# Packed attention and two mixture layers on one core: the order of all operations from a table in the kernel instead of a planner's run

## The chip, the cores and the metric

The kernel runs on one core of a Trainium2 chip. The metric is the device time of one execution in microseconds (us), as a median of several runs. Profiles are of one execution. The engines are TensorE (PE in the rows, PEld for its weight loads), VectorE (DVE), ScalarE (ACT), GpSimd (POOL) and SyncE (SP). DMAs are issued from SP's queue and, for a few tensors, from ACT's.

## The reference

```python
# q, k, v: 8 x 8 x 576 x 64; p: 8 x 8 x 32 x 64
packed = softmax(p @ k.T / 8) @ v              # 32 packed rows for each head
x = softmax(q @ packed.T / 8) @ packed         # 8 x 8 x 576 x 64 -> 4608 x 512
h = x @ moe_w_in                               # 4608 x 1024
solu = h * softmax(h)
x = layernorm(solu) * moe_g_ln @ moe_w_out     # 4608 x 512
h = x @ moe2_w_in                              # 4608 x 2048
out = relu(h) ** 2 @ moe2_w_out                # 4608 x 512
```

The weights arrive as 64-bit floats, and the kernel decodes them from their bits on ACT, DVE and POOL.

## The kernel before

**Stages.** Attention goes batch by batch (`pack`, `unpack`): scores of the packed rows against k (`s`, L648), softmax (`mx`, `nmx`, `e`), transposes of `e` (`pt`, L713), the product with v (`ppp`, L724), the packed result scaled (`pp`, `pd`, L728 and L730) and transposed (`ptp`, L740 and L741) into `ppf` and `ppq`, and scores of q against it (`s` again, L648, turned by DVE into `a` at L757). The product of `a` with the packed values and w_in is made as `G` = `ppq` times w_in (`pg`, L659, copied by ACT at L525) and `h` = `aT` times `G` (`ph`, L819 and L842), by 128 tokens. `h_tile` applies the softmax, the normalisation and transposes (`ptv`, L886), and `y_stage` multiplies by w_out (`py`), 256 tokens at a time, and stores to `y_dram`. These three run interleaved up to some 480 us. Beside them `prepare` decodes the second layer's first weights, forms seven combinations of their quarters (Strassen's products) and stores them in `z_dram`. Then come the second layer's two stages: `z_group` (seven products for a group, L1087, with sums and squares in `finish`) up to some 820 us, and `o_products` (L1221) to the end. The big products are made of three fp32r matmuls each (L543 to L545).

**The beginning.** `load_w_in` loads four parts of w_in (`wraw`, 1 MB each, one row of 8 KB on each of 128 partitions), which are decoded by three ACT instructions (L558, L565, L567) and four DVE instructions (L569, L572, L574, L577). w_out comes in the same way in four parts, with eight multiplications on ACT besides (L610, `gain`). `load_turned` loads k and q in halves of 576 KB (`kr`, `qr`), which DVE transposes (L634). `p` comes in four small DMAs (`pr`, rows of 256 B), for the first batch from ACT's queue, and DVE transposes it into `pT` (L670).

**What sets the order.** `Plan.op` and `Plan.either` only record operations: 5198 of them, each with the engines that may do it, a planned time on each, an urgency, what it reads and writes. `Plan.order` then runs through them as a list scheduler, with planned times, DMA rates and free buffers, and returns the order in which they are emitted; `Plan.backward` derives urgencies from the end; `emit` repeats both 24 times, adds the 126 `NUDGES` (shifts of urgency for stretches of the list), and emits the last order. Each engine executes its instructions in the order of their emission, and SP and ACT issue their DMAs in it too. Operations given to `either` with two engines (most weight preparations: POOL or DVE; `finish`: DVE, or ACT with two instructions, L1103 and L1104) get the one that is free first. Tiles of a shared ring (PSUM's four banks `m` among them) get the slot that came free first.

```python
order = self.order()
with self.tc.manual_schedule():
    for i in order:
        self.ops[i].fn(self.ops[i].engine)
```

Of the kernel before, what the change touches and what calls it, by code (L numbers as in the profile page):

```python
# [22 lines left out]
NUDGES = (  # L23
    (1586, 1862, DVE, -1.11), (723, 1022, DVE, -1.47), (2336, 2361, DMA, 9.02), (2358, 2372, DVE, 9.56), (696, 741, PE, 4.72),
    (870, 1143, PE, -0.81), (1028, 1040, DVE, -6.49), (1783, 1837, None, 16.47), (236, 431, DVE, -0.6), (1536, 1538, None, 2.54),
    (1591, 1756, ACT, -4.01), (1484, 1626, None, -3.27), (2001, 2027, None, -13.45), (1816, 2088, DMA, -6.41), (167, 178, None, -0.94),
    (796, 835, ACT, 1.33), (1985, 2076, DMA, 3.89), (691, 739, None, -54.14), (1771, 1847, DVE, 6.28), (1995, 2049, None, -76.95),
    (480, 683, DVE, 19.6), (487, 528, DVE, -5.08), (538, 780, ACT, -17.25), (1720, 1862, ACT, -3.92), (1626, 1631, None, -25.73),
    (472, 474, ACT, -4.98), (1610, 1852, DMA, -0.72), (2269, 2346, DMA, -5.22), (1846, 2199, PE, 18.2), (2172, 2184, PE, -1.08),
    (445, 529, None, -0.5), (945, 1021, None, -1.58), (1010, 1055, DVE, 3.0), (2218, 2282, PE, 1.4), (1086, 1271, DVE, 7.73),  # L30
    (2277, 2307, DVE, -5.99), (916, 993, DMA, 25.12), (871, 887, DVE, 18.48), (1168, 1178, DVE, -2.23), (1119, 1173, DVE, -3.12),
    (860, 884, ACT, 9.92), (2188, 2193, None, -2.05), (2273, 2344, PE, 1.65), (2308, 2377, ACT, -1.56), (258, 266, DVE, -10.26),
    (2224, 2347, None, 0.59), (642, 729, None, -2.11), (2299, 2315, None, 1.75), (831, 896, DVE, 0.82), (2031, 2195, PE, 1.46),
    (2293, 2428, DVE, 9.0), (269, 385, PE, -1.52), (662, 850, DVE, -0.09), (780, 828, None, 1.11), (1736, 1763, DMA, -0.48),
    (1792, 1825, DVE, 0.4), (1374, 1423, PE, -20.54), (261, 297, None, -1.17), (335, 423, ACT, -1.17), (1137, 1417, DVE, 9.8),
    (998, 1120, DVE, 3.18), (853, 954, DVE, -1.49), (1801, 1865, None, 14.94), (452, 458, None, -9.15), (68, 112, DVE, -2.26),
    (25, 26, None, 1.6), (157, 207, DVE, 1.98), (1290, 1377, None, -3.16), (1762, 1763, None, 13.71), (1569, 1632, DVE, 3.47),
    (4, 353, PE, -1.94), (280, 289, None, 2.49), (1590, 1594, DVE, 2.4), (1896, 1995, None, 2.54), (262, 279, None, 3.07),
    (430, 463, None, 1.29), (637, 768, ACT, 36.7), (356, 378, None, -0.85), (540, 542, DVE, -2.6), (1141, 1153, DVE, -25.46),
    (1159, 1162, PE, -9.93), (333, 359, DVE, -5.17), (752, 757, None, 2.49), (882, 1114, None, 0.41), (793, 885, DVE, 8.18),  # L40
    (643, 664, None, 3.28), (966, 1002, DVE, 36.52), (93, 99, None, -5.09), (683, 706, None, 2.3), (1789, 1853, None, -11.75),
    (257, 263, None, -9.55), (235, 371, DVE, -0.85), (206, 383, None, -0.39), (440, 448, None, -3.81), (279, 432, ACT, 6.21),
    (501, 506, None, -2.21), (269, 273, ACT, 7.19), (2124, 2127, PE, -18.82), (223, 263, DVE, -5.29), (2240, 2253, None, 1.9),
    (2096, 2277, DVE, -3.83), (412, 430, DVE, 7.08), (118, 139, None, 0.28), (1764, 1793, None, 8.76), (2211, 2492, None, 9.02),
    (2270, 2298, None, 1.31), (2204, 2587, DVE, 8.62), (2401, 2457, PE, 4.01), (2112, 2113, None, 2.19),
# [75 lines left out]
class Plan:  # L121

    WINDOW = 3413.0
    FLYING = 8
    YIELD = 60.0
    SWITCH = {True: 157.0, False: 157.0}  # L130

    @staticmethod
    def hop(a, b):

        return 0 if a == b == PE else (260, 130, 110, 70, 40)[a] + (20 if b == PE else 0)

# [45 lines left out]
    def reset(self):  # L182
        for o in self.ops:
            o.engine = None
            for b in o.bufs:
                b.slot = None
                if b.ring:
                    b.ring.free = [(0.0, n) for n in range(b.ring.bufs)]

    def backward(self):  # L190

        ops, ends = self.ops, self.ends
        deps = [set(o.deps) for o in ops]
        slots = {}
        for b in dict.fromkeys(b for o in ops for b in o.bufs if b.slot is not None):
            slots.setdefault((b.ring, b.slot), []).append(b)
        for bufs in slots.values():
            bufs.sort(key=lambda b: ends[b.touched[0]])
            for a, b in zip(bufs, bufs[1:]):
                deps[b.touched[0]].update(a.touched)  # L200
        left = [0] * len(ops)
        for i, d in enumerate(deps):
            d.discard(i)
            for j in d:
                left[j] += 1
        able = [[] for _ in range(5)]
        busy = [False] * 5
        free, starts = [0.0] * len(ops), [0.0] * len(ops)
        port = 0.0
        events = [(0.0, i, "ready") for i in range(len(ops)) if not left[i]]  # L210
        heapq.heapify(events)
        while events:
            now = events[0][0]
            while events and events[0][0] <= now:
                t, i, what = heapq.heappop(events)
                e = ops[i].engine
                if what == "ready":
                    heapq.heappush(able[e], (-ends[i], i))
                    continue
                busy[e] = False  # L220
                for j in sorted(deps[i]):
                    left[j] -= 1
                    free[j] = max(free[j], t + self.hop(ops[j].engine, e) + ops[j].lag + ops[j].slack)
                    if not left[j]:
                        heapq.heappush(events, (free[j], j, "ready"))
            for e in (PE, ACT, POOL, DVE, DMA):
                if not busy[e] and able[e]:
                    _, i = heapq.heappop(able[e])
                    busy[e] = True
                    starts[i] = now + ops[i].engines[e]  # L230
                    if e == POOL or e == DVE and ops[i].port:
                        port = starts[i] = max(now, port) + ops[i].engines[e]
                    heapq.heappush(events, (starts[i], i, "free"))
        end = max(starts)
        for o, t in zip(ops, starts):
            if not o.fixed:
                o.urgency = round((end - t) / 1e3, 6)

    def order(self):
        ops = self.ops  # L240
        self.reset()
        self.ends = [0.0] * len(ops)
        users = [[] for _ in ops]
        left = [len(o.deps) for o in ops]
        able = [[] for _ in range(5)]
        busy = [False] * 5
        events = []
        uses = {}
        pe_busy, pe_warm = {}, [False]
        port = 0.0  # L250
        landed = []

        def pe_end(t, ns):

            while ns > 1e-6:
                w = int(t / self.WINDOW + 1e-9)
                while len(pe_warm) <= w:
                    share = pe_busy.get(len(pe_warm) - 1, 0.0) / self.WINDOW
                    pe_warm.append(share > 0.74 or (share > 0.5 and pe_warm[-1]))
                slow = 1 if pe_warm[w] else 2  # L260
                d = min(ns * slow, (w + 1) * self.WINDOW - t)
                pe_busy[w] = pe_busy.get(w, 0.0) + d
                t += d
                ns -= d / slow
            return t

        for i, o in enumerate(ops):
            for d in o.deps:
                users[d].append(i)
            for b in o.bufs:  # L270
                uses[b] = uses.get(b, 0) + 1
            if not o.deps:
                heapq.heappush(events, (0.0, i, "ready"))
        order = []
        mode = [False]

        def claim(i, held, now):
            need = {}
            for b in ops[i].bufs:
                if b.ring and b.ring.shared and b.slot is None:  # L280
                    need.setdefault(b.ring, []).append(b)
            for ring, bufs in need.items():
                if sum(f <= now for f, _ in ring.free) - held.get(ring, 0) < len(bufs):
                    for r, bs in need.items():
                        held[r] = held.get(r, 0) + len(bs)
# [1027 lines left out]
```

## Time and profile before

| what | us |
|---|---|
| median of 3 runs (1199.88 to 1206.17) | 1203.17 |
| the profiled execution, its own time | 1204.65 |
| its span, first to last instruction | 1202.9 |
| PE busy | 1157.2 |
| DVE busy | 885.2 |
| ACT busy | 794.6 |
| POOL busy | 143.7 |

The profiled execution's time holds 1.75 us beyond its span. Busy time of PE includes matmuls that run at a lowered clock and pipelined ends, so the rows of single stretches say more than the sum.

### The profile page before, as it was taken

Reading aid. Unit: us, or ns where it says so; the run is one execution under the profiler, and the core shown is the slowest. Engines: PE = TensorE matmul, PEld = TensorE weight load, DVE = VectorE, ACT = ScalarE, POOL = GpSimd, SP = SyncE. Lnnn points to the kernel's source line nnn. Section 1 sums busy time; section 2 is a strip of 40 time slices with the busy share of each in tenths; the row PEclk is TensorE's granted clock in tenths of the full one; section 3 lists DMA queues with packets and bytes.
Section 4 is the critical chain, followed back from the end, with each engine's and each line's share of the span. In section 5 each row is a group of like instructions: output and inputs, shape, how many; then the busy total and the mean of one; then the engine's idle time right before and its main releaser. Section 6 shows DMA issues by size and latency. Waiting matters only on the chain.

```text
span 1202.9 us, 26204 instructions
## 1 busy us (share of the span) xinstructions
PE 1157.2 (96%) x10044; PEld 1086.8 (90%) x10044; DVE 885.2 (74%) x1784; ACT 794.6 (66%) x1672; POOL 143.7 (12%) x159
## 2 busy tenths in 40 slices
PE   1789999999999999999999999999999999999998
PEld 0357988889798999999999999999999999999998
DVE  5999897897765843567767776744888888888885
ACT  5698757776666864678777878877545454545452
POOL 0112333243232740000000000000000000000000
PEclk9789999999999999999999999999999999999999
DMA  9643563473324579677575767556983626252601
GB/s 343 199 133 118 154 195 115 149 221 119 96 76 123 154 246 356 216 243 232 190 250 189 236 203 246 169 192 239 400 320 97 190 75 186 79 187 80 189 17 54
DMA packets 171079, 218.79 MB, mean 182 GB/s; under 512 B 17353, under 2 KB 133577, under 8 KB 170185
## 3 DMA queue, kind: packets, MB, share of 16 engines
q1 hardware_dynamic: 129961, 192.07, 48.4%
q10 hardware_dynamic: 40992, 25.04, 6.8%
q8 instruction: 79, 1.29, 0.4%
q14 instruction: 47, 0.39, 0.1%
HBM read 131.08 MB, written 85.98 MB: 180 GB/s over the span
## 4 chain that ended last, share of the span: by engine, by line
PE 88%; ACT 4%; DVE 4%; DMA 2%; issue 1%; POOL 0%; ACTq 0%; SPq 0%; DVEq 0%; POOLq 0%
PE px L543 10%; PE px L545 10%; PE px L544 10%; PE ph L842 8%; PE py L543 5%; PE pa L545 5%; PE pa L543 5%; PE pa L544 5%; PE py L545 5%; PE py L544 5%; PE pz L545 3%; PE pz L543 3%; PE pz L544 3%; PE ptv L886 2%; PE s L648 2%; PE pw L544 1%
## 5 line engine op out<-in xcount | busy, mean ns | idle before, releaser
L525 ACT CAST cb<-ga 128x384 fp32r<-128x384 f32 x336 | 167.8, 514 | 161.1 <-PE pa L545 69.9
L528 DVE TENSOR_TENSOR cb<-ga,cb 128x384 fp32r<-128x384 f32 x336 | 180.4, 553 | 57.7 <-ACT cb L525 56.2
L543 PE MATMUL py<-v,wo 128*128 128x256 f32 x576 | 166.3, 289 | 0.0
L545 PE MATMUL py<-v,wo 128*128 128x256 f32 x576 | 162.8, 283 | 0.0
L544 PE MATMUL py<-v,wo 128*128 128x256 f32 x576 | 162.7, 283 | 0.0
L543 PE MATMUL px<-oi,cb 128*128 128x256 f32 x504 | 142.1, 282 | 0.8 <-ACT gw L1122 0.8
L545 PE MATMUL px<-oi,cb 128*128 128x256 f32 x504 | 142.2, 282 | 0.0
L543 PE MATMUL pa<-oi,cb 128*128 128x256 f32 x504 | 142.0, 282 | 0.0
L544 PE MATMUL pa<-oi,cb 128*128 128x256 f32 x504 | 142.0, 282 | 0.0
L545 PE MATMUL pa<-oi,cb 128*128 128x256 f32 x504 | 142.0, 282 | 0.0
L544 PE MATMUL px<-oi,cb 128*128 128x256 f32 x504 | 142.0, 282 | 0.0
L543 PE MATMUL px<-y,zi 128*128 128x384 f32 x384 | 129.6, 337 | 1.4 <-ACT gw L1091 1.3
L545 PE MATMUL px<-y,zi 128*128 128x384 f32 x384 | 129.4, 337 | 0.0
L544 PE MATMUL px<-y,zi 128*128 128x384 f32 x384 | 129.4, 337 | 0.0
L1095 DVE TENSOR_TENSOR gw<-pz,gw 128x384 f32<-128x384 f32 x96 | 53.1, 554 | 86.4 <-PE pz L545 62.1
L543 PEld LDWEIGHTS py<-v,wo 128*128 128x128 f32 x576 | 110.0, 191 | 3.0 <-DVE a L757 0.9
L544 PEld LDWEIGHTS py<-v,wo 128*128 128x128 f32 x576 | 110.2, 191 | 1.1 <-issue 0.2
L545 PEld LDWEIGHTS py<-v,wo 128*128 128x128 f32 x576 | 110.1, 191 | 0.0
L1035 DVE TENSOR_TENSOR ga<-ga 128x384 f32<-128x384 f32 x192 | 100.4, 551 | 2.1 <-DMA ga<-g_dram 1.1
L543 PEld LDWEIGHTS px<-oi,cb 128*128 128x128 f32 x504 | 95.4, 189 | 1.0 <-ACT gw L1122 1.0
L545 PEld LDWEIGHTS px<-oi,cb 128*128 128x128 f32 x504 | 95.4, 189 | 0.1
L544 PEld LDWEIGHTS px<-oi,cb 128*128 128x128 f32 x504 | 95.4, 189 | 0.0
(141 smaller groups left out, 2869.5 us busy)
## 6 DMA issues: line engine op xcount, KB each, us to landing
g_dram<-gw SPq DMA_DIRECT2D x192, 192.0 KB
ga<-g_dram SPq DMA_DIRECT2D x96, 384.0 KB
zi<-z_dram SPq DMA_DIRECT2D x28, 512.0 KB
oi<-o_dram SPq DMA_DIRECT2D x24, 512.0 KB
kr<-in_k_dram SPq DMA_DIRECT2D x16, 576.0 KB
qr<-in_q_dram SPq DMA_DIRECT2D x16, 576.0 KB
vr<-in_v_dram SPq DMA_DIRECT2D x16, 576.0 KB
y_dram<-ysb ACTq DMA_DIRECT2D x72, 128.0 KB
```

Source lines behind the costliest of these rows:

```text
L525: plan.op(ACT, c_act(cols, sbuf=r[0].pool not in (psm, psh, pso)), at, lambda: nc.scalar.copy(out_(), in_()), r=r, w=w)
L528: plan.either(on(cols, *engines), at, lambda e: vec[e].tensor_tensor(out_(), in_(), hi_().bitcast(F32), op=ALU.subtract), r=r, w=w, port=i ...
L543: nc.tensor.matmul(ps, lh, rh, start=first, stop=False, skip_group_check=onto)
L544: nc.tensor.matmul(ps, lh, rl, start=False, stop=False, skip_group_check=onto)
L545: nc.tensor.matmul(ps, ll, rh, start=False, stop=last, skip_group_check=onto)
L648: nc.tensor.matmul(banks[u]()[32 * e:32 * e + 32, :SH].rearrange("p (m t) -> p m t", t=T), lhs(ps, e, f), ts[e // 2]()[ps, e % 2, :, f], s ...
L842: nc.tensor.matmul(ph()[:, fs], al[l]()[:, g], g_tiles[b, g]()[:, r, fs], start=ends[0] and g == 0 and t == 0, stop=ends[1] and g == NG - ...
L886: nc.tensor.transpose(pt()[:, c * P:(c + 1) * P], e()[:, (4 * t + c) * P:(4 * t + c + 1) * P], ident)
L1035: plan.op(DVE, c_dve(cols), at, lambda: nc.vector.tensor_tensor(out_(), in0(), in1(), op=op), r=r, w=w, port=True)
L1095: plan.op(DVE, c_dve(HN), when(p, SN), lambda: nc.vector.tensor_tensor(t(), ps()[:, :HN], t(), op=ALU.add), r=[t, ps], w=[t])
```

## The change

The scheduler (`order`, `backward`, `reset`, the constants and `NUDGES`) is gone. `ORDER` is a table of all 5198 operations in the order of their emission, and `SECOND` lists those that go to the second of the engines that they name. The list of operations, their instructions and their buffers are as before. The lines of all that follows the tables lie 13 higher.

```diff
-NUDGES = (
-    (1586, 1862, DVE, -1.11), (723, 1022, DVE, -1.47), (2336, 2361, DMA, 9.02), (2358, 2372, DVE, 9.56), (696, 741, PE, 4.72),
...
+ORDER = (
+    45, 0, 4, 6, 53, 46, 47, 5, 48, 3, 2, 1, 382, 49, 17, 50, 61, 7, 54, 51, 55, 8, 69, 52,
...
+SECOND = (
+    1773, 1774, 1776, 1778, 1791, 1792, 1795, 1807, 1808, 1824, 1842, 1844, 1861, 1863, 1892, 1927, 1929, 1943, 1944, 1945, 1960, 1962, 1963, 1965,
...
-    def emit(self, passes):
-        order = self.order()
...
+    def emit(self):
+
+        assert sorted(ORDER) == list(range(len(self.ops))), "the table is of another list"
+        second = set(SECOND)
+        free, uses = {}, {}
         for o in self.ops:
             for b in o.bufs:
+                if b.ring and b.ring.shared:
+                    uses[b] = uses.get(b, 0) + 1
+        done = set()
+        with self.tc.manual_schedule():
+            for i in ORDER:
+                o = self.ops[i]
+                assert o.deps <= done, "the table breaks a dependence"
+                for b in o.bufs:
+                    if b in uses and b.slot is None:
+                        b.slot = free.setdefault(b.ring, list(range(b.ring.bufs))).pop(0)
+                o.fn(list(o.engines)[i in second])
+                done.add(i)
+                for b in o.bufs:
+                    if b in uses:
                         uses[b] -= 1
+                        if not uses[b]:
+                            free[b.ring].append(b.slot)
...
-    plan.emit(PASSES)
+    plan.emit()
```

Against the order before, 95 operations change their engine: 37 weight preparations of the z stage go from POOL to DVE (8 at L577, 8 of 256 and 13 of 128 columns at L925, 8 at L528), 45 `finish` operations go from ACT (35 with two instructions there, 10 with one) to one instruction on DVE, and 13 go from DVE to ACT. On PE 605 of the 1072 operations stand at the same place, and an operation moves by 1.5 places in the mean; PE's last 467 operations, ACT's last 542 and DVE's last 749 are the same list in the same order.

SP's queue from its first DMA on, before (`wraw` from w_in are the four parts of w_in):

```order
L470 DMA g_sb<-in_moe_g_ln_dram 128x8x1
L512 DMA wraw<-in_moe_w_in_dram 128x2048
L512 DMA kr<-in_k_dram 128x2x576 x2
L512 DMA wraw<-in_moe_w_in_dram 128x2048
L512 DMA qr<-in_q_dram 128x2x576 x2
L512 DMA wraw<-in_moe_w_in_dram 128x2048
L512 DMA vr<-in_v_dram 128x2x576
L512 DMA wraw<-in_moe_w_in_dram 128x2048
L512 DMA wraw<-in_moe_w_out_dram 128x8x256
```

And with the table:

```order
L483 DMA g_sb<-in_moe_g_ln_dram 128x8x1
L525 DMA wraw<-in_moe_w_in_dram 128x2048
L525 DMA kr<-in_k_dram 128x2x576 x2
L525 DMA wraw<-in_moe_w_in_dram 128x2048
L525 DMA qr<-in_q_dram 128x2x576
L525 DMA wraw<-in_moe_w_in_dram 128x2048 x2
L525 DMA qr<-in_q_dram 128x2x576
L525 DMA vr<-in_v_dram 128x2x576
L525 DMA wraw<-in_moe_w_out_dram 128x8x256
```

The third and fourth part of w_in moved ahead of the second half of q.

ACT's queue where the first batch's `G` is copied, before (`G_544` and `G_548` are the two head groups, each of two halves; `wx_265` is the first part of w_out):

```order
L525 COPY G_544<-pg_521 128x512
L525 COPY G_548<-pg_526 128x512
L525 COPY ah_130<-aT_542 128x64
L525 COPY G_544<-pg_532 128x512
L525 COPY G_548<-pg_537 128x512
L525 COPY eT_568<-pt_554 128x384
L610 ACTIVATE wx_265<-wx_265,g_neg_77 128x128 x8
L525 COPY eT_568<-pt_561 128x384
```

And with the table, with the `e` and `a1` before them (`G_534` and `G_548` are the two head groups):

```order
L709 ACTIVATE e1_497,sm1_507<-s1_468,nmx1_503 128x9x32
L793 ACTIVATE a1_439<-a1_439 128x576
L538 COPY G_534<-pg_509 128x512
L538 COPY G_534<-pg_523 128x512
L538 COPY G_548<-pg_514 128x512
L623 ACTIVATE wx_252<-wx_252,g_neg_77 128x128 x8
L538 COPY ah_391<-aT_567 128x64
L538 COPY G_548<-pg_528 128x512
L538 COPY eT_582<-pt_540 128x384
```

The last of the four copies now stands behind the eight multiplications, and one `a1` ahead of all four.

ACT's queue where the z stage begins, before (`y1` to `y7` are high parts of its operands, from two halves `yr`; `gw<-px` copies a product of a group, L1091):

```order
L525 CAST y7_6794<-yr_6662 128x384
L512 DMA y_dram5_84<-ysb_6772 128x256
L525 CAST y5_6798<-yr_6676 128x384
L1091 COPY gw_6811<-px_6787 128x384
L512 DMA y_dram5_84<-ysb_6775 128x256
L525 CAST y3_6823<-yr_6662 128x384
L525 CAST y4_6826<-yr_6662 128x384
L525 CAST y6_6829<-yr_6676 128x384
L525 CAST y7_6838<-yr_6676 128x384
L1091 COPY gw_6841<-px_6815 128x384
```

And with the table:

```order
L538 CAST y5_6810<-yr_6674 128x384
L922 COPY ysb_6814<-py_6689 128x256
L538 CAST y6_6827<-yr_6674 128x384
L538 CAST y7_6841<-yr_6674 128x384
L538 CAST y4_6844<-yr_6659 128x384
L1104 COPY gw_6847<-px_6781 128x384
L538 CAST y3_6850<-yr_6659 128x384
L1104 COPY gw_6861<-px_6803 128x384
L1104 COPY gw_6864<-px_6817 128x384
L538 CAST y3_6867<-yr_6674 128x384
```

The casts of `y6` and `y7` from both halves now stand ahead of the first copy of a product, and one cast lies between the first copy and the next two.

## Rows read from the trace of the kernel before

**Rows 1.** Waits of PE: engine, line, waited for: us, times, longest us.
```profile
PE s L648 <- DVE pT L670: 18.7, 1, 18.7
PE pt L713 <- ACT e L696: 8.8, 1, 8.8
PE px L543 <- ACT gw L1091: 1.3, 1, 1.3
```
**Rows 2.** Stretches: us, then busy by engine with count, PEclk, DMA share, GB/s.
```profile
60.00:100.00 40.00, 36.64 (x564) 22.85 (x564) 38.25 (x72) 36.12 (x81) 7.35 (x7) 0.91 0.47 149
200.00:300.00 100.00, 99.81 (x1215) 86.60 (x1209) 84.48 (x176) 67.83 (x147) 38.95 (x40) 1.00 0.49 151
500.00:600.00 100.00, 100.00 (x576) 100.00 (x575) 63.02 (x125) 77.02 (x161) 0.00 (x0) 1.00 0.66 219
...
81.50:87.00 5.50, 5.50 (x19) 3.97 (x20) 5.13 (x9) 5.33 (x15) 0.00 (x0) 0.50 0.01 3
```
**Rows 3.** DVE in order of time: start, us, instruction, idle before and releaser.
```profile
18.15 0.45 DVE L670 STREAM_TRANSPOSE pT<-pr 128x256 f32<-128x256 f32 x1 [3.30 <-DMA pr<-in_p_dram]
38.43 0.34 DVE L730 TENSOR_SCALAR pd<-ppp,rs 128x128 f32<-128x128 f32 x1
38.69 1.37 DVE L634 STREAM_TRANSPOSE kT<-kr 128x1152 f32<-128x1152 f32 x1
...
44.03 1.18 DVE L569 SCALAR_TENSOR_TENSOR wx<-wx,wraw 128x1024 int32<-128x1024 int32 x1
```
**Rows 4.** DMA queues, 13 to 14 us (first two rows), 15 to 16 us: packets, MB, share.
```profile
q1 hardware_dynamic: 137, 0.30, 91.9%
q10 hardware_dynamic: 139, 0.03, 17.1%
...
q1 hardware_dynamic: 57, 0.39, 100.8%
q10 hardware_dynamic: 55, 0.01, 6.7%
```
**Rows 5.** ACT in order of time, from 39 to 82 us.
```profile
39.18 1.23 ACT L567 ACTIVATE wraw<-wraw,mbig 128x1024 int32<-128x1024 f32 x1
40.32 0.34 ACT L525 COPY ppf<-ptp 128x256 f32<-128x256 f32 x1
...
56.34 2.45 ACT L610 ACTIVATE wx<-wx,g_neg 128x128 f32<-128x128 f32 x8
80.78 0.52 ACT L696 ACTIVATE e<-s,nmx 128x288 f32<-128x288 f32 x1
```
**Rows 6.** PE in order of time, from 39 to 84 us.
```profile
39.16 0.30 PE L741 MATMUL ptp<-ident,pp 128*128 128x128 f32 x1
40.72 3.44 PE L648 MATMUL s<-qT,ppf 32*32 32x288 f32 x64 [1.25 <-ACT ppf L525]
43.80 4.39 PE L648 MATMUL s<-kT,pT 32*32 32x288 f32 x64
50.97 4.12 PE L659 MATMUL pg<-wi,ppq 64*32 64x512 f32 x32 [2.79 <-ACT e L696]
56.69 3.60 PE L819 MATMUL ph<-G,aT 128*128 128x512 f32 x8
81.45 2.17 PE L886 MATMUL ptv<-ident,e 128*128 128x128 f32 x8 [2.96 <-ACT e L696]
```
**Rows 7.** ACT at the start of the z stage.
```profile
485.43 1.75 ACT L525 CAST y<-yr 128x384 fp32r<-128x384 f32 x4 [0.83 <-DVE yr L1035]
487.08 0.47 ACT L1091 COPY gw<-px 128x384 f32<-128x384 f32 x1
```
**Rows 8.** Groups by line: names, shapes, count; busy us, mean ns; idle before.
```profile
L528 POOL TENSOR_TENSOR wx<-wx,wh 128x896 fp32r<-128x896 f32 x16 | 34.7, 2169 | 12.8 <-ACT wh L525 12.8
...
L528 DVE TENSOR_TENSOR wx<-wx,wh 128x896 fp32r<-128x896 f32 x16 | 17.4, 1088 | 12.1 <-ACT wh L525 12.1
L1100 DVE SCALAR_TENSOR_TENSOR gw<-gw 128x384 f32<-128x384 f32 x30 | 16.7, 556 | 1.4 <-ACT gw L1122 0.7
...
L1104 ACT ACTIVATE gw<-gw 128x384 f32<-128x384 f32 x162 | 85.2, 526 | 5.1
```

More of the change, by code (lines that the diff above doesn't have):

```diff
@@ L1 @@
-import heapq
 from contextlib import ExitStack
@@ L20 @@
 PE, ACT, DVE, POOL, DMA = range(5)
-NUDGES = (
-    (1586, 1862, DVE, -1.11), (723, 1022, DVE, -1.47), (2336, 2361, DMA, 9.02), (2358, 2372, DVE, 9.56), (696, 741, PE, 4.72),
[L25 to L45, printed above, removed]
@@ L46 @@
+ORDER = (
[217 rows of a table added]
+)
+SECOND = (
[7 rows of a table added]
 )
@@ L121 @@
 class Plan:
[L127 to L135, printed above, removed]
     def __init__(self, tc):
@@ L180, in either @@
         self.ops.append(Op(engines, urgency, fn, lag, bufs, deps, port))
-    def reset(self):
+    def emit(self):
+        assert sorted(ORDER) == list(range(len(self.ops))), "the table is of another list"
+        second = set(SECOND)
+        free, uses = {}, {}
         for o in self.ops:
-            o.engine = None
             for b in o.bufs:
[L186 to L285, printed above, removed]
-                    return False
-            for ring, bufs in need.items():
-                for b in bufs:
-                    b.slot = ring.free.pop(0)[1]
-            return True
-        def take(e, t, keep=True):
-            nonlocal port
-            back, held = [], {}
-            if e == DMA and len(landed) >= self.FLYING and landed[-self.FLYING] > t:
-                if able[e] and not busy[e]:
-                    heapq.heappush(events, (landed[-self.FLYING], -1, "wake"))
-                return
-            while not busy[e] and able[e]:
-                item = heapq.heappop(able[e])
-                i = item[1]
-                o = ops[i]
-                if o.engine is not None:
-                    continue
-                if port > t + self.YIELD and (e == POOL or e == DVE and o.port):
-                    back.append(item)
-                    heapq.heappush(events, (port, -1, "wake"))
-                    continue
-                if not claim(i, held if keep else {}, t):
-                    back.append(item)
-                    continue
-                o.engine = e
-                busy[e] = True
-                order.append(i)
-                if e == POOL or e == DVE and o.port:
-                    port = self.span = max(t, port) + o.engines[e]
-                elif e == PE:
-                    ns = o.engines[e]
-                    if o.tiled != mode[0]:
-                        ns += self.SWITCH[o.tiled]
-                        mode[0] = o.tiled
-                    self.span = pe_end(t, ns)
-                else:
-                    self.span = t + o.engines[e]
-                self.ends[i] = self.span
-                if e == DMA:
-                    landed.append(self.span + 2200.0)
-                heapq.heappush(events, (self.span, i, "free"))
-                heapq.heappush(events, (self.span + o.lag, i, "done"))
-            for item in back:
-                heapq.heappush(able[e], item)
-        while events:
-            now = events[0][0]
-            while events and events[0][0] <= now:
-                t, i, what = heapq.heappop(events)
-                if what == "wake":
-                    continue
-                o = ops[i]
-                if what == "ready":
-                    for e in o.engines:
-                        heapq.heappush(able[e], (o.urgency, i))
-                elif what == "free":
-                    busy[o.engine] = False
-                else:
-                    for b in o.bufs:
-                        uses[b] -= 1
-                        if not uses[b] and b.slot is not None:
-                            b.ring.free.append((t + 200, b.slot))
-                            heapq.heappush(events, (t + 200, i, "wake"))
-                    for j in users[i]:
-                        left[j] -= 1
-                        if not left[j]:
-                            heapq.heappush(events, (t + min(self.hop(o.engine, e) for e in ops[j].engines), j, "ready"))
-            for e in (PE, ACT, POOL, DVE, DMA):
-                take(e, now)
-            if not events:
-                for e in (PE, ACT, POOL, DVE, DMA):
-                    take(e, now, False)
-        assert len(order) == len(ops), "the plan is stuck"
-        return order
@@ L363, in emit @@
-    def emit(self, passes):
-        order = self.order()
-        best, kept = max(self.ends), None
-        for _ in range(passes):
-            self.backward()
-            urgencies = [o.urgency for o in self.ops]
-            order = self.order()
-            if max(self.ends) < best:
-                best, kept = max(self.ends), urgencies
-        if kept:
-            for o, u in zip(self.ops, kept):
-                o.urgency = u
-        for i0, i1, engine, later in NUDGES:
-            for o in self.ops[i0:i1]:
-                if engine is None or next(iter(o.engines)) == engine:
-                    o.urgency += later
-        order = self.order()
-        with self.tc.manual_schedule():
-            for i in order:
-                self.ops[i].fn(self.ops[i].engine)
+                if b.ring and b.ring.shared:
+                    uses[b] = uses.get(b, 0) + 1
@@ L435 @@
     SUBS = ()
-    PASSES = 24
     AHEAD = 0.0
```

222 rows, old and new, of tables (ORDER, SECOND) are left out of this document.

## The prediction

> **What bounds the kernel now.** First comes the list of PE's waits, then the stretches of the span, then single engines in order of time. Of PE's waits the three in the list that matter are the first scores (18.7 us for `pT`), `pt` (8.8) and one of 1.3 at 485 us [rows 1]; the rest lie before 82 us too and are seen in order of time. The stretches say the same: from 60 to 100 us PE is busy for 36.64 of 40, from 200 to 300 for 99.81 of 100, from 500 to 600 for all of it, at a granted clock of 1.00 [rows 2]. So after some 82 us the kernel is PE's own work, which the change does not touch; an order can win or lose only in the first 82 us, at 485 us, or by making PE wait where it does not wait now. In the beginning the bound is not PE but VectorE: it waits 3.30 us for the small p loads, starts at 18.15 and has hardly a gap until `pd` ends at 38.77 [rows 3]. ScalarE takes that part over from 56 us on: the `e` that PE waits 2.96 us for starts only at 80.78, though its scores were done by 78.5 [rows 5, 6].
>
> The sum is made against the profiled execution's 1204.65 us (span 1202.9 and 1.75 around it), which stands 1.48 above the median of 1203.17; the forecast is brought down by that.
>
> **The change, part by part.** *The p loads.* Three of the four p loads are issued on ACT's queue behind the first w_in decode, which the table leaves there; they are 384 rows of 256 B. Beside q halves of 2304 B rows they went through at 139 packets in a microsecond, beside w_in rows of 8 KB at 55: the two queues alternate packet for packet (137 to 139, 57 to 55) [rows 4]. Before, both q halves (512 rows) lay beside them; with the table only the first half does, then the third and fourth part of w_in. The first half has some 140 of its 256 rows left at 12 us, when p begins, and is through by 12.9, with some 70 of p's rows. The other 314 pair with 256 rows of w_in, 2.1 MB at 0.40 MB in a microsecond, 5.2 us, and with 58 of the next q half, 0.4. That is 18.5, against 17 before, so `pT` starts near 19.6 instead of 18.15: **+1.45**. Bounds: 0, if p finds the queue as before, and 2.6, if it has to let the whole second q half (256 rows at 137, 1.9 us) pass too.
>
> The Trainium skill, DMA: Bandwidth & Descriptors, section on queues, rings and completion order, says that an engine goes round its queues by whole packets of about 9 to 17 descriptors. By that rule p's rows would leave in bursts, pass one w_in part at most and be done earlier than before. The trace does not agree: one for one in both stretches [rows 4].
>
> *Up to the second scores.* Between `pT` and `pd` DVE has the same instructions in both orders, in 20.6 us without a gap [rows 3]. The table puts ACT's decode of the fourth w_in part ahead of the first `e`, into time that ACT idled, and the first row maxima ahead of a decode; so PE's wait of 8.8 for `pt` [rows 1] shrinks, but what comes of it waits for `pd`, which ends at 40.2. The +1.45 passes. Then a gain: the copy of `ppf` stood behind an L567 that ended at 40.41, while `ptp` was done at 39.46 [rows 5, 6]; with the table it stands ahead of that L567. `ptp` ends 0.7 after `pd`, at 40.9, and the scores start at 41.35 instead of 40.72: **+0.6** is left.
>
> *The second batch's scores.* From 38.69 to 44.03 DVE does two transposes of k, two decodes, `pT` and the two transposes that free PSUM banks [rows 3]. The table puts the L569 of 44.03 ahead of the last three, 1.1 us more. So those scores can start at 40.2 + 5.3 + 1.1 = 46.6 instead of 43.80. Before, they were held up while they ran (4.39 where 64 of them alone took 3.44) [rows 6]; now they should run through to 50.1 against 48.2. Behind them only one maximum, `nmx` and one `e` are left on the way, where it took 2.8 before; `pg` starts at 51.2 to 51.8 instead of 50.97, **+0.5**.
>
> *The copies of G.* The last of four now stands behind one `a1` and the eight multiplications of 2.45 us [rows 5]. `pg` ends at 55.6, `pt` takes 1.8, the first half of `ph` 1.8 more: PE needs the last copy at 59.2. ACT has it ready near 59.1. It costs between 0 and 2.45; I take **+0.3**, as PE's own work covers nearly all of it.
>
> *To the end of the beginning.* From 56 to 87 us ACT has the same work but for one `a1`, which the table moves behind the `e` of 80.78. So that `e` comes with the shift of 0.8, and PE's wait of 2.96 stays about as it is. After it PE ran at a granted clock of 0.50, the lower of its two levels (1.2 and 2.4 GHz), from 81.5 to 87 [rows 2]; those 5.5 us cost 2.75, and a wait at another moment may make that stretch shorter or longer. I take no change, bounds 2.75 to both sides. The beginning thus ends at **+0.8**.
>
> *The z stage.* PE's wait of 1.3 at 486 us [rows 1] is for a copy of a product that started at 487.08, behind four casts that ACT could not start before 485.43 [rows 7]. With the table the casts of `y6` and `y7` are done before the first of these copies, and PE has three products of other groups and half a `py` between the product and its successor. **-1.3**; bounds -1.3 and 0.
>
> *The 95 operations with another engine.* Of the 37 moved from POOL, the largest takes 2169 ns there and 1088 on DVE [rows 8]. By their neighbours on DVE, 7 fall between 100 and 150 us, 7 between 150 and 300, 23 between 300 and 480. Taking each at 1.09 us at most, DVE gains under 8 us in 200 that are 16% idle [rows 2], and PE has no wait there. The net 32 of `finish` cost DVE 556 ns each, 18 us in all, in a stage where it is busy for 63%, and relieve ACT, busy for 77%, of up to two instructions of 526 ns each [rows 2, 8]. Cost: nothing, covered by PE's own work. Without that cover it would be the rival of DVE below.
>
> *The rest.* From PE's last 467 operations on, nothing moves on PE, ACT and DVE.
>
> Sum: +0.8 - 1.3 = -0.5, 1204.15 for a profiled execution, **1202.7** for the median.
>
> **The rivals.** *The wait at 79 us goes.* If ACT and DVE come to that `e` 3 us earlier, PE's 2.96 and the half clock behind it, 2.75, go, and with them the 0.8: 6.5 less, 1196.2. For it: PE has room for it, and moving one `a1` away is a step there. Against it: ACT is busy for 5.3 of the 5.5 us after it, and its work up to that `e` is otherwise the same.
>
> *p in bursts.* If p's rows pass only one w_in part, they end at 12.9 + 2.6 = 15.5 us, 1.5 earlier than before instead of 1.45 later: 3 less, 1199.7. It is what the skill's rule above would do; rows 4 speak against it.
>
> *The last copy of G decides* (slower). It does so once the second half of `ph` waits over 1 us for it, that is if `pg` ends after 56.5. Then the 2.45 of the eight multiplications lie open, the +1.45 of the p loads is no longer absorbed (0.65 more than in the sum), and a wait of that length brings the half clock, as the one of 2.96 did, for 2.75 or more. In all 2.15 + 0.65 + 2.75 = 5.6 more, 1208.3, and 1209.5 if the stretch at half clock is half as long again. For it: every step from `pT` to `pg` is late here. Against it: L610 needs 2.45 and PE has 3.6 of work.
>
> *DVE becomes the bound between 150 and 300 us.* It is at 84.48 of 100 [rows 2]; seven operations of 1.09 us at most, all open, give 7.6 us, 1210.3. Against it: PE shows no wait there.
>
> **How the numbers follow.** The forecast has 0.58, the wait that goes 0.20, bursts 0.08, the copy of G 0.10, DVE 0.04. A measurement of this kernel can tell about 0.5%, 6.0 us, from no change: faster is below 1197.2, slower above 1209.2. Faster holds the first rival but for its upper edge, and a corner of the forecast with a shorter stretch at half clock and p on time (-1.45 - 2.75 - 0.8): 0.20. Slower holds the upper half of the copy of G, DVE, and the forecast with a second stretch at half clock and the full 2.6: 0.13. The rest is 0.67. The range goes from the first rival, 1195.5 with a little more at 485 us, to the slow end of the copy of G, 1209.5.
>
> **What would show it.** In the changed profile: `pT` near 19.6, with a wait of 4.7 for the p load; `ppf` copied within 0.2 of `ptp`; `pg` after 51; no wait of PE at 485 us; one wait for an `e` near 80 and a granted clock of 0.50 after it; PE busy for all of 100 to 820 us. The forecast is wrong if PE shows a wait over 1 us after 100 us, if the clock is 1.00 from 60 to 100 us, or if `pT` starts before 18.5.

## The result and the profile after

The changed kernel takes **1210.38 us** (median of 6 runs, 1208.76 to 1211.0) against 1203.67 for the kernel before on the same chip: a ratio of **1.0051, with a 95% interval of 1.0036 to 1.0066**. It is slower by some 6.7 us, where the forecast was 1202.7 and the range ended at 1209.5. The profiled execution took 1210.16 (span 1208.2).

PE executes the same matmuls in both kernels, so an instruction that has the same set of PE operations ahead of it in both orders tells by its start how much later PE is at that point. Six of these, in the trace of before, PE in order of time (start, us, instruction):

```profile
50.97 1.08 PE L659 MATMUL pg<-wi,ppq 64*32 64x512 f32 x4 [2.79 <-ACT e L696]
115.90 0.28 PE L543 MATMUL py<-v,wo 128*128 128x256 f32 x1
390.87 0.27 PE L886 MATMUL ptv<-ident,e 128*128 128x128 f32 x1
466.79 0.36 PE L543 MATMUL py<-v,wo 128*128 128x256 f32 x1
527.40 0.34 PE L543 MATMUL px<-y,zi 128*128 128x384 f32 x1
839.99 0.28 PE L543 MATMUL px<-oi,cb 128*128 128x256 f32 x1
```

The same six in the changed kernel, whose lines lie 13 higher:

```profile
51.89 1.08 PE L672 MATMUL pg<-wi,ppq 64*32 64x512 f32 x4 [1.52 <-ACT e L709]
117.06 0.36 PE L556 MATMUL py<-v,wo 128*128 128x256 f32 x1
392.52 0.27 PE L899 MATMUL ptv<-ident,e 128*128 128x128 f32 x1
473.55 0.28 PE L556 MATMUL py<-v,wo 128*128 128x256 f32 x1
533.00 0.33 PE L556 MATMUL px<-y,zi 128*128 128x384 f32 x1
846.67 0.28 PE L556 MATMUL px<-oi,cb 128*128 128x256 f32 x1
```

Subtracting row from row, PE is 0.92 us late at 51, 1.16 at 117, 1.65 at 392, **6.76 at 473**, 5.60 at 533 and 6.68 at 847. So the beginning costs 1.2, the stretch from 390 to 473 us costs 5.1, the start of the z stage wins 1.2 back, and the last 1.1 are lost slowly up to the start of `o_products`. The largest item is in a place that the prediction had no term for.

PE's list of waits in the changed kernel (waited for: us, times, longest), to be read against [rows 1]:

```profile
PE s L661 <- DVE pT L683: 21.9, 2, 20.6
...
PE ptv L899 <- ACT e L887: 2.9, 3, 1.2
...
PE ptv L899 <- ACT ysb L922: 1.0, 1, 1.0
PE px L556 <- ACT gw L1135: 0.8, 1, 0.8
PE px L558 <- DVE cb L541: 0.6, 1, 0.6
```

The wait of 1.3 for `gw` at 485 us is gone. New are four waits of `ptv`: three for the normalised `e` (L887), one behind `ysb`, the copy of a `py` out of PSUM. All four lie between 453 and 470 us. The stretch from 430 to 476 us (busy by engine with count, PEclk, DMA share, GB/s), before:

```profile
430.00:476.00 46.00, 46.00 (x357) 44.45 (x356) 17.48 (x34) 25.83 (x51) 7.78 (x10) 1.00 0.92 319
```

and in the changed kernel:

```profile
430.00:476.00 46.00, 42.11 (x317) 39.62 (x316) 20.61 (x39) 25.67 (x48) 5.87 (x8) 1.00 0.90 292
```

PE has no gap before and 3.9 us of gaps after, while DVE, ACT and POOL are all far from full and the DMA engines are at 0.9. ACT in order of time, in the changed kernel, shows who is late:

```profile
441.60 0.38 ACT L922 COPY ysb<-py 128x256 f32<-128x256 f32 x1
...
444.46 0.37 ACT L922 COPY ysb<-py 128x256 f32<-128x256 f32 x1 [2.29 <-DMA y_dram<-ysb]
444.52 0.34 ACTq L525 DMA_DIRECT2D y_dram<-ysb  x1
...
450.55 0.37 ACT L922 COPY ysb<-py 128x256 f32<-128x256 f32 x1 [3.44 <-DMA y_dram<-ysb]
450.82 1.12 ACT L866 ACTIVATE e<-ph,nm 128x1024 f32<-128x1024 f32 x1
450.95 0.83 ACTq L525 DMA_DIRECT2D y_dram<-ysb  x2
...
451.92 1.24 ACT L887 ACTIVATE e<-e,nb,rst 128x1024 f32<-128x1024 f32 x1
```

`ysb` has two slots. The copy of 441.60 fills one, but its store is issued only at 444.52: it stands on ACT's queue behind the next copy, which waits 2.29 us for the other slot. The copy of 450.55 needs the first slot again and so waits for the store of 444.52, 3.44 us. Everything behind it on ACT waits too, the two `e` of 450.82 and 451.92 among it, and PE gets its `ptv` at 453.21. In the table 19 of the 72 stores stand behind the next copy; in the order before there were 5.

Why a store takes 6 us is in the DMA queues (packets, MB, share). From 444.5 to 448 us, that is for 3.5 us after the issue, ACT's queue q10 sends nothing:

```profile
q1 hardware_dynamic: 383, 1.39, 100.7%
```

From 448 to 450.5 us its 144 packets go:

```profile
q1 hardware_dynamic: 250, 0.91, 88.7%
q10 hardware_dynamic: 144, 0.13, 15.1%
```

q1 is SP's queue with the loads of `zi`, 512 KB each, the weights of the z stage; 18 of them are issued from 437.67 on. The kernel before issues 20 from 437.35 on, and PE has no gap there.

### The profile page after: what moved, and what is told of

Its sections match the earlier page's. It is cut to its first block, busy times and chain, and to the rows that moved or that the text cites. A ratio compares the mean times of both kernels' runs of the same rounds, so it can differ in the third digit from the quotient of the medians.

```text
span 1208.2 us, 26067 instructions
## 1 busy us (share of the span) xinstructions
PE 1159.7 (96%) x10044; PEld 1087.5 (90%) x10044; DVE 920.6 (76%) x1853; ACT 766.4 (63%) x1618; POOL 102.7 (8%) x122
## 4 chain that ended last, share of the span: by engine, by line
PE 83%; DMA 6%; DVE 5%; ACT 4%; issue 1%; POOL 0%; ACTq 0%; SPq 0%; DVEq 0%; POOLq 0%
PE px L558 10%; PE px L556 10%; PE px L557 10%; PE ph L855 7%; PE pa L556 5%; PE pa L558 5%; PE pa L557 5%; PE py L556 4%; PE py L558 4%; PE py L557 4%; DMA y_dram<-ysb 3%; PE pz L556 3%; PE pz L558 3%; PE pz L557 3%; PE ptv L899 2%; PE s L661 2%
## 5 line engine op out<-in xcount | busy, mean ns | idle before, releaser
L1104 ACT COPY gw<-px 128x384 f32<-128x384 f32 x144 | 66.7, 476 | 47.9 <-PE px L558 36.9
L556 PEld LDWEIGHTS px<-oi,cb 128*128 128x128 f32 x504 | 95.4, 189 | 1.0 <-ACT gw L1135 1.0
L558 PEld LDWEIGHTS px<-oi,cb 128*128 128x128 f32 x504 | 95.4, 189 | 0.8 <-DVE cb L541 0.8
```

What stands on the lines that cost most here:

```text
L556: nc.tensor.matmul(ps, lh, rh, start=first, stop=False, skip_group_check=onto)
L558: nc.tensor.matmul(ps, ll, rh, start=False, stop=last, skip_group_check=onto)
L1104: plan.op(ACT, c_act(HN), when(p, SN), lambda: nc.scalar.copy(t(), ps()[:, :HN]), r=[ps], w=[t])
```

## Experiments

Theory 1: the 5 us are lost because stores stand behind the next copy on ACT's queue, while the zi loads make each store slow. Rival 2: the zi loads alone do it, wherever the stores stand. Rival 3: DVE, with 37 more operations, is late.

**Stores ahead of the next copy.** ACT's queue, one of 19 places:

```diff
 L922 COPY ysb<-py 128x256
 L879 ACTIVATE den<-se,dbias 128x1
 L874 ACTIVATE ph,vs<-e,nmu 128x1024
+L525 DMA y_dram<-ysb 128x256
 L922 COPY ysb<-py 128x256
 L538 CAST v<-ptv 128x4x128
 L887 ACTIVATE e<-e,nb,rst 128x1024
-L525 DMA y_dram<-ysb 128x256
```

> The changed table, but each of the 19 y_dram stores that stand behind the next ysb copy on ACT's queue now stands just before that copy; nothing else moves. Theory 1 (the loss at 450 to 472 us comes from this place: a store is queued behind a copy that itself waits for the store before it, so the two slots of ysb work as one): ACT's wait of ysb for y_dram between 430 and 476 us falls from 11.1 us to under 6, PE's waits for e at 453, 463 and 468 go, 3.5 to 4.8 us less, 1205.6 to 1206.9. Rival 2 (the zi loads beside it make every store take 5 us, whatever the place): ACT waits as before, within 1 us of 1210.4. Rival 3 (DVE, with 37 more operations, is what is late): no change either.

Measured: 1206.6 us, ratio to before 1.0026 (1.0016 to 1.0037), against 1.0051 for the changed kernel. PE's waits from 430 to 480 us, and what ACT's copies of `ysb` waited for from 430 to 476:

```profile
PE ptv L899 <- ACT e L887: 1.0, 1, 1.0
PE ptv L899 <- ACT ysb L922: 0.2, 1, 0.2
```

```profile
  DMA y_dram<-ysb: 7.7, 5
```

PE's gaps fall from 3.9 to 1.2 us, though ACT still waits 7.7 of the 11.1 us. The third of the six instructions starts at 393.14 here and the fourth at 471.37:

```profile
471.37 0.28 PE L556 MATMUL py<-v,wo 128*128 128x256 f32 x1
```

So PE loses 2.3 us between the two, against 5.1 in the changed kernel. The place of the stores is more than half of the loss, not all of it; the ACT wait did not fall below 6, as it should have.

**One half each.** The first with the changed table for its first 1800 operations and the order of before for the rest, the second the other way round:

```diff
-    for i in ORDER:
+    for i in AFTER[:1800] + [i for i in BEFORE if i not in AFTER[:1800]]:
```

```diff
-    for i in ORDER:
+    for i in BEFORE[:1826] + [i for i in AFTER if i not in BEFORE[:1826]]:
```

> The changed table for its first 1800 operations (to some 415 us), and the order and engines of before for all that is left. Theory 1: the 1.6 us that the changed kernel has lost by 415 us stay, nothing is lost at 450 to 472, the wait of 1.3 at 485 us is back: 1203.7 + 1.6 = 1205.3. Rival 3 (the loss is made early, by DVE or by the p loads, and only shows at 450): 1208 or more.

> The order and engines of before for their first 1826 operations (to some 415 us), and the changed table for all that is left. Theory 1: 4.8 lost at 450 to 472, 1.5 won at 485, 0.8 lost at 520 to 640 and 0.8 at 843: 4.9 more than before, 1208.6. Rival 3: within 1 us of 1203.7.

Measured: 1207.89 (1.0040, 1.0028 to 1.0053) and 1207.01 (1.0031, 1.0019 to 1.0043). The second fits in kind, with a smaller loss: PE's waits from 415 to 480 us are the same two as in the changed kernel, 1.9 us for `e` (L887) and 0.8 behind `ysb`.

The first is a miss. It loses nothing from 440 to 476, where PE has no gap, but 2.3 us right at the seam, where POOL, at 18.50 of 25 us, works off weight preparations that the two orders place differently:

```profile
415.00:440.00 25.00, 22.68 (x175) 21.43 (x174) 16.82 (x31) 18.17 (x37) 18.50 (x20) 1.00 0.60 170
```

PE waits there for ACT, 1.2 us behind `ysb` and 1.1 for `e`; that POOL's work is the reason is not shown. So an order cut in two makes a loss of its own. On the early part the trace sides with theory 1, though the total is near rival 3's 1208: at the third of the six instructions (392.14) PE is 1.3 late.

**The second half of q early.** SP's queue:

```diff
-L525 DMA qr<-in_q_dram 128x2x576
+L525 DMA qr<-in_q_dram 128x2x576 x2
 L525 DMA wraw<-in_moe_w_in_dram 128x2048 x2
-L525 DMA qr<-in_q_dram 128x2x576
```

> The changed table with one DMA moved on SP's queue: the second half of q again ahead of the third part of w_in, as before. Theory of the prediction (p's rows pair with 8 KB rows of w_in): pT starts at 18.2 to 18.6 instead of 20.12, and the 1.2 us that PE is late at 57 us fall to 0 to 0.4: 1209.2 to 1209.6. Rival (the third and fourth part of w_in come later and their decode gives it back): pT early, but PE at 57 us as late as in the changed kernel, 1210.4 or more. Rival 2 (p waits for something else): pT stays at 20.

Measured: 1207.94 (1.0038, 1.0025 to 1.0052). `pT` starts at 18.36, 1.76 earlier than in the changed kernel, where the forecast had 1.45, and the first `pg` of PE starts at 50.14 instead of 51.89. So the later half of q does set p's time, and the fourth part of w_in gives nothing back. The total is below the 1209.2 to 1209.6 that were expected, but its interval takes them in; PE still has 3.3 us of gaps from 440 to 476.

**Stores behind the next copy, in the order of before.** The reverse of the first run: of the change alone this, for seven stores between 437 and 470 us.

```diff
 L922 COPY ysb<-py 128x256
-L525 DMA y_dram<-ysb 128x256
 L874 ACTIVATE ph,vs<-e,nmu 128x1024
 L538 CAST wh<-wx 128x896
 L538 CAST v<-ptv 128x4x128
 L525 DMA z_dram<-wh 128x7x128
 L922 COPY ysb<-py 128x256
+L525 DMA y_dram<-ysb 128x256
```

> The order of before as a table, with one thing of the change alone: seven y_dram stores between 437 and 470 us now stand on ACT's queue just behind the next ysb copy instead of ahead of it. Theory 1 (store behind the next copy makes the two slots work as one): ACT's wait for y_dram between 430 and 476 us grows from 9.0 us to 12 or more, PE waits for e or ptv in that stretch, 2 to 4.8 us more, 1205.5 to 1208. Rival (the place of a store is harmless while PE has other work): within 1 us of 1203.3.

Measured: **1214.01, 1.0078 (1.0064 to 1.0093)**, 10 us more, over twice what was expected. ACT's wait of `ysb` and PE's waits from 430 to 476 us:

```profile
  DMA y_dram<-ysb: 16.0, 6
```

```profile
PE ptv L899 <- ACT ysb L922: 2.9, 1, 2.9
PE ptv L899 <- ACT e L887: 2.3, 1, 2.3
```

These waits are 5.2 of the 10 us. The expectation had no term for PE's granted clock, which fell to 0.50 behind the wait of 2.9, and again at the start of the z stage, behind a wait for `gw` that is 1.9 here and was 1.3 before:

```profile
452.30:455.70 3.40, 3.40 (x18) 3.40 (x18) 0.00 (x0) 0.00 (x0) 0.00 (x0) 0.50 1.03 412
496.70:500.10 3.40, 3.40 (x12) 3.40 (x12) 1.91 (x4) 3.06 (x8) 0.00 (x0) 0.50 0.77 251
```

Half of 3.4 us, 1.7, is lost in each of the two. Together with the 0.6 more for `gw` that makes 9.2, and PE is 9.6 late at the fifth of the six instructions (537.03). In the changed kernel the clock stayed at 1.00 in this stretch. Seven DMA issues, moved by a few places on a queue where they block nothing by themselves, cost more than the whole change.

**w_in early, in the order of before.** SP's queue:

```diff
-L525 DMA qr<-in_q_dram 128x2x576 x2
-L525 DMA wraw<-in_moe_w_in_dram 128x2048
-L525 DMA vr<-in_v_dram 128x2x576
-L525 DMA wraw<-in_moe_w_in_dram 128x2048
+L525 DMA qr<-in_q_dram 128x2x576
+L525 DMA wraw<-in_moe_w_in_dram 128x2048 x2
+L525 DMA qr<-in_q_dram 128x2x576
+L525 DMA vr<-in_v_dram 128x2x576
```

> The order of before, with the third and fourth part of w_in issued ahead of the second half of q on SP's queue, as in the changed kernel, and nothing else. If p's rows pair with w_in's: pT at 19.6 to 20.2 instead of 18.15, PE's first scores 1.5 to 2 later, and since DVE has no gap until pd, PE at 57 us 1.3 to 2 later: 1204.6 to 1205.2. Rival: q's later half or DVE's gaps absorb it, below 0.5 more.

Measured: 1205.26, 1.0014 (1.0005 to 1.0023): 1.7 more. `pT` starts at 20.15, 2.0 later than in [rows 3], and `pg` at 52.97 is 2.0 later too: with a DVE that has no gap until `pd`, all of it passes.

**The mended versions.** Since DVE waits for p and nothing else there, p can simply go first (ACT's queue):

```diff
+L525 DMA pr<-in_p_dram 32x4x64
+L485 ACTIVATE g_neg<-g_sb 128x8
+L525 DMA pr<-in_p_dram 32x4x64 x3
 L840 CAST ah<-zero 128x2x64
...
-L525 DMA pr<-in_p_dram 32x4x64
-L485 ACTIVATE g_neg<-g_sb 128x8
...
-L525 DMA pr<-in_p_dram 32x4x64 x3
```

> The order of before with the four p loads of the first batch issued first on ACT's queue, from its operation 2038 on (some 470 us) the changed table, and 5 stores put ahead of the next copy. If p is what DVE waits for at 14.85 us: pT starts there, 3.3 earlier, and PE at 57 us is 2 to 3.3 earlier; the wait of 1.3 at 485 us is gone, 0.8 to 1.2 lost later in the z stage: 1200 to 1201.5. Rival (w_in or k come later behind p and take the gain): PE at 57 us as before, 1202.5 to 1203.5.

Measured: **1198.57, 0.9956 (0.9943 to 0.9970)**, faster than both kernels.

```profile
14.78 0.44 DVE L683 STREAM_TRANSPOSE pT<-pr 128x256 f32<-128x256 f32 x1
```

`pT` runs 3.37 earlier without a wait, and PE's `pg` starts at 47.62, 3.35 earlier. The rest of the 5 us is not the p loads' alone: the run has the changed z stage too. The changed table with the three mends together:

> The changed table with three mends: p loads first on ACT's queue, the second half of q ahead of the third part of w_in, the 19 stores ahead of the next copy. Theory 1: from the changed kernel's 7 us over before, 3.2 to 4.8 go at 450 to 472 and 3 to 5 in the beginning: 1201.5 to 1204. Rival (what is gained early is lost at 450 to 476 again, as in the run with q early, where DMA sets the pace): 1206 to 1208.

Measured: 1201.62, 0.9986 (0.9974 to 0.9997), 8.8 below the changed kernel. From 430 to 480 us PE has one wait left, 1.4 us for `e` (L887).

**The engines of before in the changed order.**

```diff
-SECOND = (the 167 operations of the changed kernel)
+SECOND = (the 162 operations that the planner gave to their second engine)
```

> The order of the changed table, but each of the 95 operations on the engine that it had before (37 weight preparations back on POOL, 45 operations of finish back on ACT, 13 back on DVE). The prediction put these 95 at nothing: 1210.4, within 1 us, and PE's waits at 453, 463 and 468 us stay. Rival (the 37 operations on DVE make the stretch to 472 us late): 3 to 5 less, 1205.4 to 1207.4. Rival 2 (the order was made for these engines, so POOL is now late with them): PE waits in 300 to 440 us, 1211.5 or more.

Measured: 1217.16, 1.0106 (1.0086 to 1.0126), 6.8 more than the changed kernel. From 400 to 480 us POOL is busy for 35.01 us, where it was for 14.60 in the changed kernel, and ACT waits for it:

```profile
ACT wh L538 <- POOL wx L938: 7.3, 3, 3.8
```

In the changed kernel this wait is 0.4. So POOL is late in an order that was not made for it: the second rival of this run. A new loss hides here whatever an old one gave back, so this run does not say what the 37 operations cost on DVE. Rival 3 falls by others: the order of before with the stores deferred has these operations on POOL and loses more, and the first run has them on DVE and loses less.

**Only the start of the z stage.** As the run with p first, but from operation 2087 on (some 490 us) again the order of before.

```diff
-    for i in E7:
+    for i in E7[:2087] + [i for i in BEFORE if i not in E7[:2087]]:
```

> As the run with p first and the z stage of after, but the order and engines of before come back from operation 2087 on (some 490 us), so that only the start of the z stage is the changed table's. If the wait at 485 us goes with that start, and the 0.6 to 0.8 lost later belong to the rest of the changed z stage: 1197.5 to 1198.2. Rival (the start of the z stage pays back in its first groups what it wins): 1198.6 to 1199.5.

Measured: 1199.49, 0.9960 (0.9945 to 0.9976). This is the upper end of the rival's range, and it can't be told from 1198.57 by the medians. The traces say more. The fifth and the sixth of the six instructions, here:

```profile
523.49 0.34 PE L556 MATMUL px<-y,zi 128*128 128x384 f32 x1
836.08 0.28 PE L556 MATMUL px<-oi,cb 128*128 128x256 f32 x1
```

and in the run with p first, which keeps the changed z stage:

```profile
522.33 0.33 PE L556 MATMUL px<-y,zi 128*128 128x384 f32 x1
836.02 0.28 PE L556 MATMUL px<-oi,cb 128*128 128x256 f32 x1
```

Between the two lie 312.59 us here, as in the kernel before, and 313.69 there, nearly as in the changed kernel (313.67). So the last 1.1 us belong to the rest of the changed z stage. That PE comes to the sixth at nearly the same time in both is partly luck: by the second instruction the run with p first was 1.55 ahead (111.03 against 112.58), with PE's clock at 0.50 for some 3.4 us near 80 us instead of 6.8, though the two have the same order up to there.

**The zi loads out of the way.** SP's queue, on top of the first run:

```diff
-L525 DMA zi<-z_dram 128x1024 x14
 L525 DMA yr<-y_dram 128x2x768 x2
+L525 DMA zi<-z_dram 128x1024 x14
```

> As the first run (19 stores ahead of the next copy), and 14 of the 18 zi loads that ran beside the stores now stand on SP's queue behind the last of the yr loads, at some 470 us. The total is not the point, since the z stage will wait for its operands; the stretch from 437 to 468 us is. If the zi loads are what makes a store take 5 us: a store there lands within 2 to 3 us, ACT's wait for y_dram between 445 and 468 us falls from some 5.7 to under 1.5, and the 1.7 us that PE still lost there in the first run fall to 0.5 or less. Rival (the rest is the order of ACT or PE itself): PE's waits for e and ptv stay at 1.3 and 0.2, and 1.7 are lost as before. In both cases PE then waits for zi, 15 us or more: 1222 or more.

Measured: 1221.57 (1.0152, 1.0119 to 1.0184), since the z stage now waits for its weights. In the stretch itself PE has no gap left:

```profile
430.00:476.00 46.00, 46.00 (x357) 44.37 (x356) 20.53 (x39) 25.41 (x48) 5.86 (x8) 1.00 0.49 147
```

```profile
  DMA y_dram<-ysb: 3.7, 2
```

Both waits that are left (2.5 and 1.2 us, at 445.15 and 448.81) lie at the end of the four zi loads that stayed. A store then goes at once: the one issued at 454.54 sends all its 144 packets before 456. The third of the six instructions starts at 392.65 and the fourth at 469.27:

```profile
469.27 0.28 PE L556 MATMUL py<-v,wo 128*128 128x256 f32 x1
```

So 0.7 us are lost between them. Theory 1 holds in both of its parts: of the 5.1 us 2.8 go with the place of the stores and another 1.6 with the zi loads; 0.7 stay open. What late zi loads do while the stores stand behind the next copy was not run.

## Why the prediction was wrong

**What failed.** The prediction said that an order can win or lose only in the first 82 us, at 485 us, "or by making PE wait where it does not wait now". For this last case it priced the 95 moved operations and nothing else, and it closed the list with "The rest", which speaks only of what lies behind the z stage's start. The order of ACT's queue from 100 to 480 us had no term. It should have had one: in the trace of before ACT already waits for these stores.

```profile
  DMA y_dram<-ysb: 9.0, 4
```

(Before, the copies of `ysb` from 430 to 476 us.) PE had other work beside each of these waits, 24 matmuls of `ph` in a row beside the longest. A wait that costs nothing is a margin that a new order can use up; the forecast looked at PE's waits alone. The missing term is 5.1 us; the other parts together came to +1.6 where the forecast had -0.5. The prediction's own sign of being wrong came with it, a wait of PE over 1 us after 100 us: 1.2 at 453.21. Its reading of PE's list was not complete either: one wait of before, 0.8 for `gw` (L1122), lies at 838 us and not before 82. It stayed as it was.

**The p loads: right, a little small.** The forecast was `pT` at 19.6; it came at 20.12, so +1.97 instead of +1.45.

```profile
20.12 0.45 DVE L683 STREAM_TRANSPOSE pT<-pr 128x256 f32<-128x256 f32 x1 [5.30 <-DMA pr<-in_p_dram]
```

The queues from 14 to 15 us and from 18 to 19 us show the pairing as forecast, one for one beside w_in and beside the second half of q:

```profile
q1 hardware_dynamic: 47, 0.38, 94.7%
q10 hardware_dynamic: 47, 0.01, 5.7%
```

```profile
q1 hardware_dynamic: 143, 0.31, 84.2%
q10 hardware_dynamic: 141, 0.03, 16.0%
```

What was too small is the start: the forecast gave p some 70 rows beside the first half of q, but up to 13 us only 10 packets of q10 were sent. The 60 others, at some 141 in a microsecond, are the missing 0.4 to 0.5. The rule of the Trainium skill, DMA: Bandwidth & Descriptors, section on queues, rings and completion order, that an engine drains a whole packet of about 9 to 17 descriptors before it goes to its next queue, would have had p early; these rows speak against it again, and so that rival fell.

**Up to the first ph: right.** The second scores were to start at 46.6, `pg` at 51.2 to 51.8, the last copy of G near 59.1, the `e` at 0.8 more than 80.78 (it came at 82.00):

```profile
46.94 3.43 PE L661 MATMUL s<-kT,pT 32*32 32x288 f32 x64 [1.31 <-DVE pT L683]
```

```profile
59.04 0.58 ACT L538 COPY G<-pg 128x512 f32<-128x512 f32 x1
```

PE did not wait for G, so the rival of the copy of G did not occur, though its time of 1208.3 to 1209.5 was near the measured one. Nearer still was the rival of DVE from 150 to 300 us, with 1210.3, and it did not occur either; PE has no wait there:

```profile
150.00:300.00 150.00, 149.87 (x1985) 127.79 (x1985) 128.12 (x267) 102.88 (x228) 40.76 (x44) 1.00 0.53 163
```

That its time agrees is chance. The beginning ends 1.16 late, for a forecast of 0.8. The half clock behind the wait for the `e` stayed, as forecast, and so did the wait (3.0 us):

```profile
82.50:87.00 4.50, 4.38 (x16) 3.72 (x17) 4.50 (x8) 4.50 (x13) 0.00 (x0) 0.50 0.70 247
```

That it stayed as long is partly luck. The run with the changed table for its first 1800 operations has the same order here, but in its execution the clock is back at 1.00 before 87 us, and the second of the six instructions comes at 115.55 instead of 117.06:

```profile
82.50:87.00 4.50, 4.50 (x18) 3.21 (x18) 4.50 (x6) 4.32 (x12) 0.00 (x0) 0.62 0.60 204
```

So a part of 1 to 1.5 us, read from one execution of each kernel, can be this stretch and not the order.

**The start of the z stage: right.** -1.3 forecast, -1.2 measured, and PE's list has no wait for `gw` at this place any more.

**The 95 operations: nothing speaks against it.** Forecast at nothing. With all 95 moved, PE has no gap of note from 100 to 430 us, and none from 430 to 476 in the run with the zi loads late, so the 37 on DVE cost nothing there. For the `finish` operations it is not shown: the changed z stage loses 1.1 us from 533 to 847, and with them back on ACT it loses 3.4 (539.67 to 855.65), but in an order that was made for the other engines.

**Small and not forecast:** 0.5 us between 117 and 392, and 1.1 between 533 and 847, of which 0.6 is the new wait for `cb`, at 845.74. There DVE and ACT have the same list in both orders, which the prediction took for no change ("The rest").

The parts add up: 1.16 + 0.5 + 5.1 - 1.16 + 1.08 = 6.7 us, and PE's last matmul starts 6.7 us later (1204.35 against 1197.65). That the medians differ by as much is partly luck: the spans of these two executions differ by 5.3 only, because from the start of its last matmul the one of before ran on for 5.2 us and the other for 3.9.

## What to carry to other kernels

When an order changes, follow each small ring of buffers through it: with two slots, a store that is queued behind the next copy on the same engine turns the ring into one slot, and the engine then stands still for the store's landing time. That time is the one of the busiest stretch of DMA, not the usual one. Read the waits of every engine in the trace of before, also those that cost nothing there, and when an engine waits for a small load, try to issue that load first: here PE's first `pg` then started 3.35 us earlier.

## What was not expected of the hardware

A store of 128 KB on ACT's queue had sent all its packets 1.5 us after its issue when SP's queue was idle, and none 3.5 us after it when SP's queue held loads of 512 KB; then all 144 went within 2.5 us. So the busy queue cost the other one mostly a late start, which a rate of packets in a microsecond does not show. The forecast of p made the same mistake.
